# A second expert's operands prepared a block ahead, and four inverse half-products moved, in a spectral layer with two experts

## The chip, the cores and the metric

The kernel runs on one core of a Trainium2 chip. The metric is the time of one execution on the device in microseconds (us); the kernel before takes 1209.12 us, the median of 3 runs (1208.78 to 1209.31). PE is the matrix engine (PEld its weight loads), DVE the vector engine, ACT the scalar engine, POOL the GpSimd engine; SP only issues transfers.

## The reference

Two parts follow each other. The first takes x (2 x 3008 x 256), transforms it along the 3008 positions, multiplies by a complex matrix, shrinks the result towards zero and transforms back. The second sends all 6016 tokens through two dense experts with a hidden width of 2048.

```python
X = rfft(x, axis=1)
Yr = X.real @ w_r - X.imag @ w_i + b_r
Yi = X.real @ w_i + X.imag @ w_r + b_i
Y = sign(Y) * max(abs(Y) - 0.01, 0)          # real and imaginary part each
x = irfft(Y, n=3008, axis=1).reshape(6016, 256)
h = x @ moe_w_in;   x = (h - tanh(h)) @ moe_w_out
h = x @ moe2_w_in;  return (h * clip(h + 3, 0, 6) / 6) @ moe2_w_out
```

All is float32. The kernel writes each large float32 product as three products of rounded operands: a value is split into a rounded part (hi, by an ACT copy) and a remainder (lo, by a subtraction on DVE or POOL), and `three_pass` adds hi x hi, hi x lo and lo x hi.

## The kernel before

The front (lines 649 to 787) does the transform in steps A to D. A and B are matmuls into the frequency domain, `linear` the complex matrix, `shrink` the threshold, C and D the way back. A loop over t = 0 to 23 runs `linear(t)`, `dft_c(t-2)` and `dft_b(t+2)` together; C's results go to DRAM and come back by `load_din(i)`, and `dft_d(i, dh)` is one inverse half-product: eight PE matmuls as the trace counts them into one PSUM bank, then an ACT copy (line 419) into one of the four blocks B11, B12, B21, B22 of a token block.

Then come 16 token blocks k: 0 to 7 for the first expert (752 tokens each, two halves of 376) and 8 to 15 for the second (640, then 768 each, halves of 320 and 384). Each block runs 8 groups g, one for each 256 columns of the hidden layer. A group computes the 2 x 2 block product of weights and tokens with seven products instead of eight (p1 to p7), on operands that `op_split` prepares once per token block: b11, b21, t1, t2, b22, t3, t4, where T1 = B12 - B11, T2 = B22 - T1, T3 = B22 - B12, T4 = B21 - T2 come from `op_sub` on POOL. b11, b21, t1 and t2 have two homes, in `cmH` and `cmL`, for even and odd blocks. b22, t3 and t4 have one home each.

The order of the work is written by hand: each engine runs its instructions in the order of the program, and waits are put in for the data. `group` (line 605) issues p1, p2, p5; ACT's copy `s` of p1 (line 616); the nonlinearity `nl` and its split for the group before; then the outputs of the group before in four parts (`outp`) between p6 with p3, p7 and p4. Products p1, p6, p7 and p4 all build up in one PSUM bank `al`: p6 has to wait until `s` is copied, p7 until `su` is (line 628), p4 until DVE has added `c22` (line 637). Between these steps `hook("a")` to `hook("e")` call `super_hook`, which places everything else: weight decoding, loads, stores and the preparation of the next block n = k + 1:

```python
(5,d) T1, T2   (6,a) b11   (6,d) b21   (7,a) t1, T3   (7,b) t2, T4   (7,e) b22
(0,a) of block n: t3      (0,b) of block n: t4
```

Remainders of b11, b21, t1 and t2 run on POOL, those of b22, t3 and t4 on DVE. While block k of the first expert runs, the four half-products of block n are done at hook c of groups 2 to 5; blocks 9 to 15 load their tokens from DRAM (`load_y1`) at hook c of group 1.

`first_group` (line 574) is group 0 of block 0, cut in pieces that run between the last steps of the front, because the front's last two C products and its DVE steps are still under way.

Of the kernel before, what the change touches and what calls it, by code (L numbers as in the profile page):

```python
# [10 lines left out]
F32 = mybir.dt.float32  # L11
F32R = mybir.dt.float32r
# [76 lines left out]
def spectral_moe_kernel(ctx: ExitStack, tc: tile.TileContext, x, w_r, w_i, b_r, b_i,  # L89
# [72 lines left out]
    def w_flush():  # L162
        w_load(ptr["due"])
        ptr["due"] = 0
# [64 lines left out]
    cmH = pb.tile([128, K1 * 128], F32R, name="cmH")  # L229
    cmL = pb.tile([128, K1 * 128], F32R, name="cmL")  # L230
    b22 = [pb.tile([128, 384], F32R, name=f"b22{p}") for p in "hl"]
    bi_all = pb.tile([128, 3 * 4 * D], F32, name="bi_all")
    bi_ring = [bi_all[:, 4 * D * r:4 * D * (r + 1)].rearrange("p (k d) -> p k d", d=D) for r in range(3)]


    at = ctx.enter_context(ExitStack())
# [168 lines left out]
    def load_din(i, t=None):  # L405
        b, q = divmod(i, 8)
        if t is None:
            t = bi_ring[i % 3]
        t = t[0:96]
        sp.dma_start(out=t, in_=s2w[b][:, 4 * q:4 * q + 4, :])  # L410
        din_t[i] = t

    def dft_d(i, dh, tag):
        t = din_t[i]
        p = bank(tag)
        for u in range(4):
            pe.matmul(out=p[:, u * 94:(u + 1) * 94], lhsT=t[:, u, dh * 128:(dh + 1) * 128], rhs=dmt,  # L417
                      start=True, stop=True)
        act.activation(out=xtf[:, 2 * dh + i % 2, 0:NT].rearrange("p (r u) -> p u r", u=4),  # L419
                       in_=p[:, 0:NT].rearrange("p (u r) -> p u r", u=4), func=ACTF.Copy)  # L420

# [5 lines left out]
    def op_sub(k, out, a, b, eng=pool):  # L427
        eng.tensor_tensor(out=blkv(k, out), in0=blkv(k, a), in1=blkv(k, b), op=ALU.subtract)  # L428

    def op_hi(k, nm):  # L430
        src, slot = OPS[nm]
        n = span[k][1]
        if slot is not None:
            o = 1536 * (k % 2) + NM * slot
            h, l = cmH[:, o:o + n], cmL[:, o:o + n]
        elif nm == "b22":
            h, l = (t[:, 0:n] for t in b22)
        else:
            h, l = (mo["w"].tile([128, NM], F32R, tag=nm + p, name=nm + p)[:, 0:n] for p in "hl")
        act.activation(out=h, in_=blkv(k, src), func=ACTF.Copy)  # L440
        opnd[k, nm] = (h, l)
# [7 lines left out]
        op_lo(k, nm, eng)  # L449

    def early_slot(i):
        return bi_all[:, NT * i:NT * (i + 1)]

    def wt(tag, nt, n=1):
        return mo["w"].tile([128, NM], F32, tag=tag, bufs=n, name=tag)[:, 0:nt]
# [22 lines left out]
    def product(k, g, nm, dst, start):  # L478
        blk, op = PROD[nm]
        w = W["1i" if k < NS else "2i", g]  # L480
        h, l = opnd[k, op]
        sl = slice(blk * 128, (blk + 1) * 128)
        three_pass(dst, w[:, 0, sl], w[:, 1, sl], h, l, start, True, skip_group_check=True)
# [80 lines left out]
    def tail_nl(stage):  # L564
# [5 lines left out]
        else:  # L570
            nl_split(k, g, 1, 0, pend.pop("g"))
            pend.pop("c21")

    def first_group():
        al, be, ga = (bank(t)[:, 0:NT] for t in ("al", "be", "ga"))
        s1, c11, s5, c12, c22 = (early_slot(i) for i in range(5))
        product(0, 0, "p1", al, True)
        product(0, 0, "p2", ga, True)
        product(0, 0, "p5", be, True)
        act.activation(out=s1, in_=al, func=ACTF.Copy)  # L580
        dve.tensor_tensor(out=c11, in0=ga, in1=s1, op=ALU.add)
        act.activation(out=s5, in_=be, func=ACTF.Copy)
        yield
        nl(0, c11, True)
        yield
        product(0, 0, "p6", al, False)
        product(0, 0, "p3", be, False)
        act.activation(out=s1, in_=al, func=ACTF.Copy)
        dve.tensor_tensor(out=c12, in0=be, in1=s1, op=ALU.add)
        yield  # L590
        op_split(0, "t3")
        product(0, 0, "p7", al, False)
        op_hi(0, "t4")
        dve.tensor_tensor(out=c22, in0=al, in1=s5, op=ALU.add)
        op_lo(0, "t4")
        product(0, 0, "p4", al, False)
        nl(0, c12, True)
        nl_split(0, 0, 0, 0, c11)
        nl(0, c22, True)
        nl_split(0, 0, 0, 1, c12, pool)  # L600
        yield
        nl_split(0, 0, 1, 1, c22)
        pend["c21"] = (0, 0, al)
# [45 lines left out]
    with tc.manual_schedule():  # L649
# [61 lines left out]
        for t in range(NP):  # L711
            linear(t)
            if t > 1:
                dft_c(t - 2)
            if t + 2 < NP:
                dft_b(t + 2)
            ab = dft_a(a_next, False) if a_next < 16 else None
            if t > 1:
                evict_c(t - 2)
            if t + 2 < NP:  # L720
                evict_b_hi(t + 2)
            shrink(t)
            if t < NP - 1:
                shrink_hi(t)
            if t + 2 < NP:
                evict_b_lo(t + 2)
            if t == NP - 1:
                first = first_group()
                next(first)
                shrink_hi(t)  # L730
            if t + 2 < NP:
                evict_b_neg(t + 2)
            for _ in range(3 if t < 10 else 2):
                if t > 1 and ptr["dec"] < NDEC:
                    w_step()
            shrink_lo(t)
            for nm in {20: ("b11", "b21"), 21: ("t1",), 22: ("t2", "b22")}.get(t, ()):
                op_lo(0, nm)
            if t == 20:
                op_sub(0, "T1", "B12", "B11", dve)  # L740
            if t == 21:
                op_sub(0, "T2", "B22", "T1", dve)
            if ab:
                dft_a_out(a_next, ab)
                a_next += 1
            flush_stores()
            if t % 2 == 0:
                load_bm(t // 2 + 2)
                load_cm(t // 2 + 1, s_t[t][0].bitcast(F32)[0:1, 0, 0:1])
            if t > 0:  # L750
                load_x(10 + t)
            if t == 0:
                w_load()
            if t % 2 == 1:
                load_bi((t + 1) // 2 + 2)
            w_flush()
            for _ in range(3 if t < 10 else 1 + t % 2):
                if t > 1 and ptr["dec"] < NDEC:
                    w_step()
            if t == 14:  # L760
                load_din(0, din0)
            if t == 15:
                load_din(1, x1[2])
            if t in (17, 18):
                dft_d(0, t - 17, "h")
            if t in (19, 20):
                dft_d(1, t - 19, "h")
            for nm in {19: ("b11", "b21"), 20: ("t1",), 21: ("t2", "b22")}.get(t, ()):
                op_hi(0, nm)
            if t == 22:  # L770
                op_sub(0, "T3", "B22", "B12", dve)
                op_sub(0, "T4", "B21", "T2", dve)

        next(first)
        dft_c(NP - 2)
        next(first)
        evict_c(NP - 2)
        flush_stores()
        dft_c(NP - 1)
        w_flush()  # L780
        at.close()
        mo["w"] = ctx.enter_context(tc.tile_pool(name="mw", bufs=1, reuse_waits="tile"))
        next(first)
        evict_c(NP - 1, bi_all[:, 6 * NT:6 * NT + 512].rearrange("p (k d) -> p k d", k=2))
        flush_stores()
        for _ in first:
            pass

        def super_hook(k, g, pos):
            n = k + 1  # L790
            if g == 0:
                if pos == "a":
                    op_split(k, "t3")
                if pos == "b":
                    op_split(k, "t4")
                if pos == "d":
                    finish(k - 1, 0)
                if pos == "e":
                    finish(k - 1, 1)
            if pos == "a":  # L800
                flush_stores()
            if n < 2 * NS:
                if n < NS:
                    if g == (k == 0) and pos == "c":
                        load_din(2 * n)
                        load_din(2 * n + 1)
                    if 2 <= g < 6 and pos == "c":
                        dft_d(2 * n + (g - 2) // 2, g % 2, "ga")
                elif g == 1 and pos == "c":
                    load_y1(n)  # L810
                if g == 5 and pos == "d":
                    op_sub(n, "T1", "B12", "B11")
                    op_sub(n, "T2", "B22", "T1")
                if g == 6 and pos == "a":
                    op_split(n, "b11", pool)
                if g == 6 and pos == "d":
                    op_split(n, "b21", pool)
                if g == 7 and pos == "a":
                    op_split(n, "t1", pool)
                    op_sub(n, "T3", "B22", "B12")  # L820
                if g == 7 and pos == "b":
                    op_split(n, "t2", pool)
                    op_sub(n, "T4", "B21", "T2")
                if g == 7 and pos == "e":
                    op_split(n, "b22")
            if 1 <= g < 6 and k < NS:
                if pos in "bcd" or pos == "a" and (k == 0 or g % 2):
                    if k or ptr["dec"] < 16:
# [56 lines left out]
```

## Time and profile before

| | |
|---|---|
| median of 3 runs | 1209.12 us |
| the profiled execution | 1207.54 us |
| its span, first to last instruction | 1205.7 us |
| PE busy | 1185.2 us (98%) |
| PEld busy | 1166.4 us (97%) |
| DVE busy | 962.7 us (80%) |
| ACT busy | 875.2 us (73%) |
| POOL busy | 158.7 us (13%) |
| mean granted TensorE clock | 0.995 |

The front ends at about 170 us, the first expert at about 691 us. Matmul records overlap, since a matmul of 376 columns starts every 0.17 us and is shown 0.34 us long; a short hole is therefore seen better in the weight loads, and in the distance between starts, than in PE's busy time.

### The profile page before, as it was taken

How to read it: one execution, taken by the hardware profiler on the slowest of the kernel's cores; microseconds unless marked ns; L12 is line 12 of the kernel's file. 1: busy time of each engine (PE TensorE's matmuls, PEld its weight loads, DVE VectorE, ACT ScalarE, POOL GpSimd, SP SyncE). 2: the span in 40 equal slices, each digit the busy share in tenths (PEclk: the TensorE clock that was granted, in tenths of full speed). 3: DMA queues.
4: the chain of work that ended last, by engine and by line, in shares of the span. 5: the costliest groups of instructions: out<-in, count | busy, mean ns of one | idle time of the engine just before them, and what ended most of it. 6: DMA issues, size and time to landing. Idle time of an engine off the chain costs nothing.

```text
span 1205.7 us, 20883 instructions
## 1 busy us (share of the span) xinstructions
PE 1185.2 (98%) x7806; PEld 1166.4 (97%) x7806; DVE 962.7 (80%) x1818; ACT 875.2 (73%) x1828; POOL 158.7 (13%) x162
## 2 busy tenths in 40 slices
PE   8999999999999999999999999999999999999998
PEld 6899989999999999999999999999999999999997
DVE  2599988888988888888777788778787878787875
ACT  2586768777777777777777677777777777777775
POOL 1010000203020110202021402020200202020200
PEclk9899999999999999999999999999999999999999
DMA  8996522112222223120105530101010101010000
GB/s 274 289 315 230 175 86 64 37 54 75 103 95 75 74 75 105 53 88 20 52 1 185 183 117 1 49 2 53 1 54 1 54 1 53 1 43 12 16 13 27
DMA packets 49149, 96.52 MB, mean 80 GB/s; under 512 B 4424, under 2 KB 28072, under 8 KB 49048
## 3 DMA queue, kind: packets, MB, share of 16 engines
q1 hardware_dynamic: 43078, 74.09, 19.2%
q0 software_dynamic: 4032, 14.68, 3.9%
q10 hardware_dynamic: 1938, 6.42, 1.5%
q8 instruction: 61, 1.00, 0.4%
q14 instruction: 40, 0.33, 0.1%
HBM read 58.22 MB, written 36.44 MB: 79 GB/s over the span
## 4 chain that ended last, share of the span: by engine, by line
PE 73%; DVE 10%; ACT 9%; DMA 5%; issue 2%; SPq 0%; ACTq 0%; DVEq 0%
PE acc L120 13%; PE acc L122 12%; PE acc L121 12%; PE al L120 7%; PE al L121 6%; PE al L122 6%; PE be L120 3%; PE be L122 3%; PE be L121 3%; DMA xb<-in_x_dram 3%; ACT gh L116 2%; PE ga L417 2%; DVE g L463 2%; PE ga L120 2%; PE ga L122 2%
## 5 line engine op out<-in xcount | busy, mean ns | idle before, releaser
L117 DVE TENSOR_TENSOR gl<-g,gh 128x376 fp32r<-128x376 f32 (+2 forms) x509 | 290.9, 571 | 149.1 <-ACT gh L116 123.3
L116 ACT ACTIVATE gh<-g 128x376 fp32r<-128x376 f32 (+2 forms) x509 | 263.0, 517 | 176.1 <-DVE g L466 91.9
L121 PE MATMUL acc<-wo,gh 128*128 128x256 f32 x752 | 211.7, 282 | 0.0
L120 PE MATMUL acc<-wo,gh 128*128 128x256 f32 x752 | 211.5, 281 | 0.0
L122 PE MATMUL acc<-wo,gl 128*128 128x256 f32 x752 | 211.1, 281 | 0.0
L120 PE MATMUL acc<-gh,wo 128*128 128x376 f32 x512 | 173.8, 339 | 0.0
L122 PE MATMUL acc<-gh,wo 128*128 128x376 f32 x512 | 171.1, 334 | 0.0
L121 PE MATMUL acc<-gl,wo 128*128 128x376 f32 x512 | 170.8, 334 | 0.0
L122 PEld LDWEIGHTS acc<-wo,gl 128*128 128x128 f32 x752 | 142.7, 190 | 0.0
L121 PEld LDWEIGHTS acc<-wo,gh 128*128 128x128 f32 x752 | 141.9, 189 | 0.0
L120 PEld LDWEIGHTS acc<-wo,gh 128*128 128x128 f32 x752 | 141.7, 188 | 0.0
L428 POOL TENSOR_TENSOR bmt<-bmt 128x376 f32<-128x376 f32 (+2 forms) x60 | 74.2, 1237 | 458.2 <-ACT bmt L419 332.2
L466 DVE SCALAR_TENSOR_TENSOR g<-e,c 128x384 f32<-128x384 f32 (+1 forms) x192 | 119.6, 623 | 11.8 <-ACT e L465 6.4
L465 ACT ACTIVATE e<-c,three 128x384 f32<-128x384 f32 (+1 forms) x192 | 116.7, 608 | 8.2 <-DVE c L630 8.0
L463 DVE TENSOR_TENSOR g<-c,e 128x376 f32<-128x376 f32 x189 | 114.1, 604 | 6.1 <-ACT e L462 3.3
L445 POOL TENSOR_TENSOR cmL<-bmt,cmH 128x376 fp32r<-128x376 f32 (+2 forms) x60 | 64.8, 1081 | 308.2 <-ACT cmH L440 308.2
L462 ACT ACTIVATE e<-c 128x376 f32<-128x376 f32 x189 | 97.4, 516 | 10.3 <-DVE c L630 10.2
L120 PEld LDWEIGHTS acc<-gh,wo 128*128 128x128 f32 x512 | 96.3, 188 | 0.0
L121 PEld LDWEIGHTS acc<-gl,wo 128*128 128x128 f32 x512 | 96.2, 188 | 0.0
L122 PEld LDWEIGHTS acc<-gh,wo 128*128 128x128 f32 x512 | 96.1, 188 | 0.0
L620 ACT ACTIVATE s<-be 128x376 f32<-128x376 f32 (+2 forms) x127 | 61.7, 486 | 39.7 <-PE be L122 38.4
L120 PE MATMUL al<-cmH,wi 128*128 128x376 f32 (+2 forms) x256 | 87.7, 343 | 2.4 <-ACT s L616 2.0
(182 smaller groups left out, 2843.5 us busy)
## 6 DMA issues: line engine op xcount, KB each, us to landing
raw<-in_moe_w_in_dram SPq DMA_DIRECT2D x16, 512.0 KB
raw<-in_moe_w_out_dram SPq DMA_DIRECT2D x16, 512.0 KB
w2id<-wout SPq DMA_DIRECT2D x8, 896.0 KB
wi<-w2id POOLq DMA_DIRECT2D x8, 896.0 KB, 4.8
y1d<-y SPq DMA_DIRECT2D x32, 188.0 KB
s<-co SPq DMA_DIRECT2D x23, 256.0 KB
bi_all<-s SPq DMA_DIRECT2D x11, 512.0 KB
bi_all<-s SPq DMA_DIRECT2D x14, 384.0 KB
```

The source lines that it names most:

```text
L116: act.activation(out=hi, in_=src, func=ACTF.Copy)
L117: (lo_eng or dve).tensor_tensor(out=lo, in0=src, in1=hi.bitcast(F32), op=ALU.subtract)
L120: pe.matmul(out=out_ap, lhsT=lh, rhs=rh, start=start, stop=False, **kw)
L121: pe.matmul(out=out_ap, lhsT=lh, rhs=rl, start=False, stop=False, **kw)
L122: pe.matmul(out=out_ap, lhsT=ll, rhs=rh, start=False, stop=stop, **kw)
L428: eng.tensor_tensor(out=blkv(k, out), in0=blkv(k, a), in1=blkv(k, b), op=ALU.subtract)
L445: (eng or dve).tensor_tensor(out=l, in0=blkv(k, OPS[nm][0]), in1=h.bitcast(F32), op=ALU.subtract)
L462: act.activation(out=e, in_=src, func=ACTF.Tanh)
L463: dve.tensor_tensor(out=g, in0=src, in1=e, op=ALU.subtract)
L465: act.activation(out=e, in_=src, func=ACTF.Relu, bias=three)
L466: dve.scalar_tensor_tensor(out=g, in0=e, scalar=6.0, in1=src, op0=ALU.min, op1=ALU.mult)
L620: act.activation(out=s5, in_=be, func=ACTF.Copy)
```

## The change

Four edits. (1) b22 gets a second home for odd blocks, and in the first expert its split moves from hook (7,e) to (6,e). (2) For blocks 9 to 15, b22, t3 and t4 have second homes in odd blocks; all seven splits are placed in groups 2 to 6 of the block before (`prep`), all with their remainders on POOL, and `load_y1` moves to group 0. (3) The four half-products of block 1 leave groups 2 to 5 of block 0: three are issued between the last pieces of the front, the fourth inside `first_group`. The two of i = 3 are only multiplied there, and their ACT copies run at hook a of group 1. Their inputs are loaded at t = 16 and t = 21 into tiles that held x. (4) The ring `bi_all` becomes three tiles, so that the second homes can follow in their place; the front's last C result goes to a tile of the experts' pool.

```diff
-    bi_all = pb.tile([128, 3 * 4 * D], F32, name="bi_all")
-    bi_ring = [bi_all[:, 4 * D * r:4 * D * (r + 1)].rearrange("p (k d) -> p k d", d=D) for r in range(3)]
+    bi_ring = [pb.tile([128, 4, D], F32, tag=f"ring{r}", name=f"bi{r}") for r in range(3)]
+    second = {}
...
+        elif k % 2 and (nm == "b22" or k > NS):
+            if nm not in second:
+                r = ("t3", "t4", "b22").index(nm)
+                second[nm] = pb.tile([128, 2, 512], F32R, tag=f"ring{r}", name=nm + "s")
+            h, l = (second[nm][:, i, 0:n] for i in range(2))
         elif nm == "b22":
...
         op_split(0, "t3")
         product(0, 0, "p7", al, False)
+        ahead.append(dft_d_mm(3, 1, "acc"))
         op_hi(0, "t4")
...
+            if t == 16:
+                load_din(2, x1[1])
+            if t == 21:
+                load_din(3, x1[2])
...
         next(first)
         dft_c(NP - 2)
+        for dh in range(2):
+            dft_d(2, dh, "acc")
         next(first)
         evict_c(NP - 2)
         flush_stores()
         dft_c(NP - 1)
+        ahead.append(dft_d_mm(3, 0, "acc"))
...
-        evict_c(NP - 1, bi_all[:, 6 * NT:6 * NT + 512].rearrange("p (k d) -> p k d", k=2))
+        evict_c(NP - 1, mo["w"].tile([128, 2, D], F32, tag="wout", name="cl"))
...
+        def prep(n, g, pos):
+            if pos == "a" and g == 4:
+                op_sub(n, "T1", "B12", "B11")
+            if pos == "a" and g == 5:
+                op_sub(n, "T2", "B22", "T1")
+                op_sub(n, "T3", "B22", "B12")
+            if pos == "e" and g == 5:
+                op_sub(n, "T4", "B21", "T2")
+            nm = {(2, "d"): "b11", (3, "d"): "b21", (4, "d"): "t1", (5, "d"): "t2",
+                  (6, "a"): "b22", (6, "c"): "t3", (6, "e"): "t4"}.get((g, pos))
+            if nm:
+                op_split(n, nm, pool)
+        def prep_early(n, g, pos):      # as before, but for b22
...
+            nm = {(6, "a"): "b11", (6, "d"): "b21", (6, "e"): "b22"}.get((g, pos))
+            if nm:
+                op_split(n, nm, None if nm == "b22" else pool)
...
-                if pos == "a":
+                if pos == "a" and k <= NS:
                     op_split(k, "t3")
-                if pos == "b":
+                if pos == "b" and k <= NS:
                     op_split(k, "t4")
...
+                if k == 0:
+                    if g == 1 and pos == "a":
+                        for dh in range(2):
+                            dft_d_out(3, dh, ahead[dh])
...
-                elif g == 1 and pos == "c":
+                elif g == (n <= NS) and pos == "c":
                     load_y1(n)
...
-                if g == 7 and pos == "e":
-                    op_split(n, "b22")
+                if n > NS:
+                    prep(n, g, pos)
+                else:
+                    prep_early(n, g, pos)
```

NS is 8. `dft_d_mm` and `dft_d_out` are the two halves of `dft_d`: the matmuls, and the ACT copy.

## Rows read from the trace of the kernel before

**Rows 1.** The page, part 1: busy us, share of the span, instructions.

```profile
PE 1185.2 (98%) x7806; PEld 1166.4 (97%) x7806; DVE 962.7 (80%) x1818; ACT 875.2 (73%) x1828; POOL 158.7 (13%) x162
```

**Rows 2.** Waits from 160 us on: who for whom, us in total, times, longest.

```profile
PEld al L120 <- ACT s L616: 6.7, 16, 1.0
```

**Rows 3.** PE in the second expert, p6 of five groups: start, us, instruction.

```profile
748.66 0.45 PE L120 MATMUL al<-cmH,wi 128*128 128x384 f32 x1 [0.83 <-ACT s L616]
...
828.94 0.34 PE L120 MATMUL al<-cmH,wi 128*128 128x384 f32 x1
...
836.90 0.34 PE L120 MATMUL al<-cmH,wi 128*128 128x384 f32 x1
...
877.03 0.44 PE L120 MATMUL al<-cmH,wi 128*128 128x384 f32 x1 [0.16 <-ACT s L616]
...
941.30 0.44 PE L120 MATMUL al<-cmH,wi 128*128 128x384 f32 x1 [0.16 <-ACT s L616]
```

**Rows 4.** PE in the first expert: p6 of four groups, and one half-product.

```profile
194.58 1.03 PE L417 MATMUL ga<-dmt,bi_all 96*128 96x94 f32 x8
195.39 0.42 PE L120 MATMUL acc<-gh,wo 128*128 128x376 f32 x1
...
565.22 0.44 PE L120 MATMUL al<-cmH,wi 128*128 128x376 f32 x1
...
631.36 0.44 PE L120 MATMUL al<-cmH,wi 128*128 128x376 f32 x1
...
654.88 0.33 PE L120 MATMUL al<-cmH,wi 128*128 128x376 f32 x1
...
662.62 0.34 PE L120 MATMUL al<-cmH,wi 128*128 128x376 f32 x1
```

**Rows 5.** ACT at the change into block 11.

```profile
875.62 0.51 ACT L440 ACTIVATE b22h<-bmt 128x384 fp32r<-128x384 f32 x1
...
876.50 0.48 ACT L616 ACTIVATE s<-al 128x384 f32<-128x384 f32 x1
```

**Rows 6.** DVE in block 10, groups 2 and 7.

```profile
831.50 1.15 DVE L466 SCALAR_TENSOR_TENSOR g<-e,c 128x384 f32<-128x384 f32 x1
...
833.87 0.56 DVE L466 SCALAR_TENSOR_TENSOR g<-e,c 128x384 f32<-128x384 f32 x1
...
872.44 0.55 DVE L637 TENSOR_TENSOR c<-al,s 128x384 f32<-128x384 f32 x1
...
873.73 1.37 DVE L466 SCALAR_TENSOR_TENSOR g<-e,c 128x384 f32<-128x384 f32 x1
```

**Rows 7.** POOL in the same two groups.

```profile
829.82 2.42 POOL L428 TENSOR_TENSOR bmt<-bmt 128x384 f32<-128x384 f32 x2 [19.40 <-DMA bmt<-y1d]
...
872.06 1.33 POOL L445 TENSOR_TENSOR cmL<-bmt,cmH 128x384 fp32r<-128x384 f32 x1
873.35 1.33 POOL L428 TENSOR_TENSOR bmt<-bmt 128x384 f32<-128x384 f32 x1
```

**Rows 8.** Two stretches: length, busy PE, PEld, DVE, ACT, POOL; clock, DMA share, GB/s.

```profile
164.50:166.20 1.70, 0.07 (x1) 0.00 (x0) 1.42 (x3) 0.61 (x2) 0.00 (x0) 1.00 0.00 0
169.90:172.90 3.00, 3.00 (x9) 2.89 (x10) 2.13 (x5) 2.23 (x6) 0.98 (x1) 0.50 0.01 3
```

**Rows 9.** PE: p4 of groups 0 and 1 of block 0.

```profile
169.87 0.65 PE L120 MATMUL al<-t4h,wi 128*128 128x376 f32 x1 [0.73 <-DVE bi_all L594]
...
179.17 0.33 PE L120 MATMUL al<-t4h,wi 128*128 128x376 f32 x1
```

**Rows 10.** ACT in the front and in group 1 of block 0.

```profile
148.11 0.86 ACT L419 ACTIVATE bmt<-ga 128x376 f32<-128x376 f32 x1
148.76 0.92 ACT L440 ACTIVATE cmH<-bmt 128x376 fp32r<-128x376 f32 x2
...
166.53 0.46 ACT L588 ACTIVATE bi_all<-al 128x376 f32<-128x376 f32 x1
...
175.26 0.48 ACT L628 ACTIVATE su<-al 128x376 f32<-128x376 f32 x1 [0.26 <-PE al L122]
```

More of the change, by code (lines that the diff above doesn't have):

```diff
@@ L407, in load_din @@
         if t is None:
-            t = bi_ring[i % 3]
+            t = bi_ring[i % 2]
         t = t[0:96]
@@ L413, in dft_d, with dft_d_mm @@
     def dft_d(i, dh, tag):
+        dft_d_out(i, dh, dft_d_mm(i, dh, tag))
+    def dft_d_mm(i, dh, tag):
         t = din_t[i]
@@ L418, in dft_d, with dft_d_out @@
                       start=True, stop=True)
+        return p
+    def dft_d_out(i, dh, p):
         act.activation(out=xtf[:, 2 * dh + i % 2, 0:NT].rearrange("p (r u) -> p u r", u=4),
@@ L451, in early_slot @@
     def early_slot(i):
-        return bi_all[:, NT * i:NT * (i + 1)]
+        return bi_ring[i // 2].rearrange("p k d -> p (k d)")[:, NT * (i % 2):NT * (i % 2 + 1)]
     def wt(tag, nt, n=1):
@@ L572, in tail_nl @@
             pend.pop("c21")
+    ahead = []
     def first_group():
@@ L787, in spectral_moe_kernel @@
             pass
+        def prep(n, g, pos):
[11 more added lines that the diff above has]
+        def prep_early(n, g, pos):
+            if (g, pos) == (5, "d"):
+                op_sub(n, "T1", "B12", "B11")
+                op_sub(n, "T2", "B22", "T1")
+            if (g, pos) == (7, "a"):
+                op_split(n, "t1", pool)
+                op_sub(n, "T3", "B22", "B12")
+            if (g, pos) == (7, "b"):
+                op_split(n, "t2", pool)
+                op_sub(n, "T4", "B21", "T2")
+            nm = {(6, "a"): "b11", (6, "d"): "b21", (6, "e"): "b22"}.get((g, pos))
+            if nm:
+                op_split(n, nm, None if nm == "b22" else pool)
         def super_hook(k, g, pos):
@@ L802, in super_hook @@
             if n < 2 * NS:
-                if n < NS:
-                    if g == (k == 0) and pos == "c":
+                if k == 0:
+                    if g == 1 and pos == "a":
+                        for dh in range(2):
+                            dft_d_out(3, dh, ahead[dh])
+                elif n < NS:
+                    if g == 0 and pos == "c":
                         load_din(2 * n)
@@ L808, in super_hook @@
                         dft_d(2 * n + (g - 2) // 2, g % 2, "ga")
-                elif g == 1 and pos == "c":
+                elif g == (n <= NS) and pos == "c":
                     load_y1(n)
[L811 to L823, printed above, removed]
-                if g == 7 and pos == "e":
-                    op_split(n, "b22")
+                if n > NS:
+                    prep(n, g, pos)
+                else:
+                    prep_early(n, g, pos)
             if 1 <= g < 6 and k < NS:
```

## The prediction

> **What bounds the kernel now.** I read the busy times first: PE works 98% of the span [rows 1], so only two things can shorten it, less PE work or fewer PE holes. Then I read the waits of PEld, because a hole shows first on the weight load that stands in front of a late matmul. After the front the largest by far is one wait: the weight load of a product into `al` waits for ACT's copy `s` (line 616), 16 times for 6.7 us, the longest 1.0 us [rows 2]. The rows at 748.66, 877.03 and 941.30, which name that wait, are each the first group of a new token block [rows 3]; followed in the order of time, 14 of the 16 are the changes into blocks 1 to 7 and 9 to 15. So the holes sit at the block changes, and in the front just before the first expert.
>
> What one block change costs is read from the starts of product p6 (first `al` matmul after the first outputs). In the second expert two neighbouring groups are 836.90 - 828.94 = 7.96 us apart, a whole block is 941.30 - 877.03 = 64.27 us, and 64.27 - 8 x 7.96 = 0.59 us is lost per block [rows 3]. At 748.66 (block 9, behind the short block 8 of 320 tokens) PE shows 0.83 us idle where the later changes show 0.16 [rows 3], so this one costs 0.59 + 0.67 = about 1.3 us. In the first expert a group is 662.62 - 654.88 = 7.74 us, an inverse half-product (`dft_d`) takes 195.39 - 194.58 = 0.81 us to the next matmul and that one is 0.08 us late, 0.89 us in all; a block with four of them is 631.36 - 565.22 = 66.14 us, so 66.14 - 8 x 7.74 - 4 x 0.89 = 0.66 us is lost per block [rows 4].
>
> Why ACT is late there: just before `s` it runs the `b22h` copy (875.62, then a tanh-like step, then `s` at 876.50) [rows 5], and it came late to that copy because DVE's `g` took 1.37 us where it takes 0.56 alone [rows 6], beside the last two of four POOL operations in a row (872.06 and 873.35, 1.33 us each) [rows 7].
>
> **The change, part by part.** *b22 a group earlier (all blocks).* One ACT copy (two steps of ACT there take 876.50 - 875.62 = 0.88, so 0.44 us for one [rows 5]) and one DVE subtract leave the block change for the end of group 6. In groups 6 and 7 `s` waits for PE, not PE for `s`: none of the 16 waits [rows 2] is in group 7, so 0.44 us is covered there. The 0.66 us of a change falls on two products, p6 (for `s`) and p7 (for t3). I give each half, an estimate: then `s` is 0.33 us late, and with 0.44 us less on ACT it is early by 0.1 us. In blocks 1 to 8 t3 and t4 stay in group 0, on ACT and DVE; they move up with ACT by the same 0.44 us, and p7 by 0.3 us, so p7 should just not wait: a margin of 0.1 us. If that cover is missing, a third of the 0.66 us stays. Bounds for the 7 changes into blocks 1 to 7: 1.5 us (p6 alone, partly) to 7 x 0.66 = 4.6 us; I take three quarters, 3.3 us. The change into block 8 has no such wait; between none and 0.6 us I take 0.2.
>
> *t3, t4, b22 of blocks 9 to 15 prepared a block ahead, remainders on POOL.* Nothing of the operand work is left in groups 7 and 0 but t4's remainder on POOL at the start of group 7, so neither the four-in-a-row nor the extra ACT copies reach the change: 6 x 0.59 = 3.5 us, and 1.3 us for block 9. What it adds is three POOL subtracts per block (1.2 to 1.3 us each [rows 7]) and a denser stretch in groups 4 to 6. POOL's queue is in order, and a subtraction that waits for nothing runs right behind its forerunner: t1's remainder, T2 and T3 run as one chain of some 3.9 us behind group 4, then t2's remainder and T4. The nearest row for such a chain is the pair at 829.82, 2.42 us long [rows 7]; DVE's `g` beside it took 1.15 us [rows 6], and the group around it (828.94 to 836.90) is the one that gave the 7.96 us [rows 3]. That pair cost PE nothing, the chain of four with an ACT copy behind it cost 0.59. A chain of three lies between, and behind it no change follows; I take zero, with 0.3 us per block (2 us) as the other end, and below nothing no gain, since the operations are only added there. The load of y1 moves one group earlier; the tile it writes was last read in group 7 or before, so it waits for nothing.
>
> Beside that: DVE's `c` (line 637), which reads PSUM, took 0.55 us beside POOL, and `g`, which reads two SBUF tiles, took 1.37 [rows 6]. The Trainium skill's page "SBUF — State Buffer", section "Who interferes with whom", says that such a DVE operation and a GpSimd operation that reads SBUF exclude each other for a whole instruction. The rows agree; by that rule alone each POOL operation more may hold up one DVE operation, which is the third rival.
>
> *Half-products of the second block to the front.* Four `dft_d` leave groups 2 to 5 of block 0: 4 x 0.89 = 3.56 us of PE time gained, if the front holds them for nothing. The front has the hole: PE works 0.07 of 1.70 us from 164.5 on [rows 8], since `dft_c(23)` waits for ACT's `sh` until past 166.2, and p4 waits until 169.87 [rows 9]. The first two (1.78 us, before p6 and p3) fill the first hole almost exactly; their two ACT evictions (0.86 us long, the next start 148.76 - 148.11 = 0.65 later [rows 10]) push ACT's copy of 166.53 [rows 10] and all behind it by 1.3 us. The third needs an `acc` bank that `evict_c(22)`, the step behind that copy, frees at about 168.8 (167.8 plus 0.4 and 0.6); it runs to 169.7, p7 follows, the fourth lies under DVE's c22, and p4 starts near 171.2 instead of 169.87. But the granted clock was 0.50 from 169.9 to 172.9 [rows 8], 1.2 GHz, after PE had idled; with the holes mostly filled I expect full clock, and the 9 matmuls counted there, 3.0 / 9 = 0.33 us each, take 7.74 / 45 = 0.17: 1.4 us back. So the first output product starts when it did. Then the bill: in group 1 ACT is still 1.4 us late and now has the third and fourth evictions (1.3 us) ahead of `su`, which ran at 175.26 [rows 10]; and the second pair of `acc` banks that the output product needs is held by them until about 177.2. `su` ends near 177.5, p7 starts near 177.9, and p4 of group 1 near 180.5 instead of 179.17 [rows 9]: 1.3 us lost. T1 and T2 now also run on POOL in this group, beside a DVE that does weight decoding: 0.3 us. Net 3.56 - 1.6 = 2.0 us; bounds -0.5 us (clock low again, 1.4, and a further 1.1 of ACT backlog) and 3.6 us. The two loads moved to SP's queue at t = 16 and 21 write tiles whose readers are done, and stand ahead only of stores and loads needed some 10 us later: nothing.
>
> **The sum.** 3.3 + 0.2 + 3.5 + 1.3 + 2.0 = 10.3 us. The profiled execution took 1207.54 us (span 1205.7), so it would take 1197.2; the median of 1209.12 lies 1.6 us above it, so 1198.8 us.
>
> **Rivals.** *A, the stall only moves (14%).* The chain of three with t1h, or t2's with b22h, does to a group inside the block what the chain of four did to the change. For: same operations, same DVE line. Against: the free pair at 829.82. Then the 4.8 us of blocks 9 to 15 are not saved: 1203.6 us. *B, the front gives nothing and p7 keeps its wait for t3 (14%).* For: ACT and DVE have no slack in group 1, and t3 stays where it was up to block 8. Against: the hole of 1.70 - 0.07 = 1.63 us is there [rows 8]. Without 2.0 and half of 3.3: 1202.5 us. *C, slower (5%).* In blocks 9 to 15 the place is DVE's `g` and `gl`: 11 POOL operations a block instead of 8, and up to 1.37 - 0.55 = 0.8 us for each. It decides once more than (10.3 / 7) = 1.5 us per block of these 11 x 0.8 = 8.8 us reaches PE; with 2 us reaching it the time is 1198.8 + 14 = 1213. Against: eight such operations a block, with three ACT copies at the change, now cost 0.59 [rows 3]. *D, the second homes or the earlier loads wait for their old users*, so that nothing moves (3%): 1209. 64% stay for the forecast, whose own range is 1195 to 1202.
>
> **How the numbers follow.** Best case: 3.6 in the front, 4.6, 0.4 and 4.8 make 13.4, plus the clock beyond my share, about 1194.5 us. Above, A and B belong in; together they reach 1207, but one alone stays under 1204. Range 1194.5 to 1204. A measurement tells 0.2% (2.4 us) from no change: forecast, A and B are faster by that: 0.91; within 0.05; slower 0.04.
>
> **What would show it.** In the trace after: no PEld wait for `s` at block changes 9 to 15, and the distance of p6 over a block 63.7 us there and 65.5 in blocks 1 to 7; `dft_d` at 163.4 and the stretch behind 169.9 at clock 1.00; a wait of 1 to 1.5 us in group 1 of block 0. Wrong: new PEld waits in groups 4 to 6 of blocks 8 to 14 (A, C), p7 waiting for t3 in blocks 1 to 7 (B), or clock 0.5 behind 169 us.

## The result, and the profile after

The changed kernel takes 1199.28 us, the median of 6 runs (1197.74 to 1202.5); the kernel before took 1208.95 in the runs beside it (1208.56 to 1213.51). The ratio is 0.9916, 95% interval 0.9901 to 0.993: 8.5 to 12.0 us less, where 10.3 were forecast. The profiled execution of the changed kernel is its longest run, 1202.5 us with a span of 1200.7, only 5.0 us under the span before. Where that comes from is the first thing to read, or every later stage looks 3.8 us worse than it is.

The page of the changed kernel, part 1, answers to [rows 1]; below it is a line of its part 5 (count, then busy us, mean ns of one, idle before).

```profile
PE 1181.7 (98%) x7806; PEld 1165.6 (97%) x7806; DVE 941.2 (78%) x1797; ACT 879.2 (73%) x1828; POOL 178.6 (15%) x183
...
L477 DVE SCALAR_TENSOR_TENSOR g<-e,c 128x384 f32<-128x384 f32 (+1 forms) x192 | 105.6, 550 | 16.2 <-ACT e L476 11.6
```

POOL got the 21 subtractions (3 for each of blocks 9 to 15) that DVE lost. Though POOL works more, DVE's `g` in the second expert is now 550 ns on the mean, and none of the 192 above takes more than 560. At the end of block 10, where [rows 6] had 1.37 us, the changed kernel's DVE shows:

```profile
871.00 0.56 DVE L477 SCALAR_TENSOR_TENSOR g<-e,c 128x384 f32<-128x384 f32 x1
872.87 0.55 DVE L477 SCALAR_TENSOR_TENSOR g<-e,al 128x384 f32<-128x384 f32 x1
...
875.19 0.56 DVE L477 SCALAR_TENSOR_TENSOR g<-e,c 128x384 f32<-128x384 f32 x1
```

The waits of PEld from 165 us on (who for whom, us in total, times, longest) answer to [rows 2]:

```profile
PEld al L120 <- ACT s L630: 1.6, 5, 0.5
PEld al L120 <- DVE c L651: 1.6, 4, 0.7
PEld acc L120 <- ACT bmt L425: 1.3, 2, 1.1
```

From 6.7 us in 16 waits, the wait for `s` (now line 630) is down to 1.6 in 5, all of them before 692 us; in the second expert PEld waits for nothing. `acc` waiting for `bmt` is new: the price of the moved half-products. PE at p6 in the second expert, for [rows 3]:

```profile
747.63 0.34 PE L120 MATMUL al<-cmH,wi 128*128 128x384 f32 x1
...
874.62 0.34 PE L120 MATMUL al<-cmH,wi 128*128 128x384 f32 x1
...
882.57 0.34 PE L120 MATMUL al<-cmH,wi 128*128 128x384 f32 x1
...
938.30 0.34 PE L120 MATMUL al<-cmH,wi 128*128 128x384 f32 x1
```

No row has a wait behind it. A block is 938.30 - 874.62 = 63.68 us, which is 8 x 7.96: the change of block costs nothing. In the first expert, for [rows 4], a block is 631.96 - 566.28 = 65.68 us instead of 66.14:

```profile
566.28 0.34 PE L120 MATMUL al<-cmH,wi 128*128 128x376 f32 x1
...
631.96 0.34 PE L120 MATMUL al<-cmH,wi 128*128 128x376 f32 x1
```

The end of the front, for [rows 8] and [rows 9]: the granted clock stays at full, and p4 of groups 0 and 1 starts at 175.02 and 184.46. In the first fence (windows) the numbers behind the length are busy PE, PEld, DVE, ACT and POOL, then the clock. The second is PE, the third ACT.

```profile
168.00:177.00 9.00, 7.95 (x51) 6.85 (x50) 6.42 (x13) 6.04 (x13) 0.16 (x1) 1.00 0.08 29
...
176.00:179.00 3.00, 3.00 (x19) 2.84 (x18) 2.13 (x5) 3.00 (x8) 0.99 (x1) 1.00 0.26 88
```

```profile
175.02 0.41 PE L120 MATMUL al<-t4h,wi 128*128 128x376 f32 x1
...
180.50 0.44 PE L120 MATMUL acc<-gh,wo 128*128 128x376 f32 x1 [0.75 <-ACT bmt L425]
...
184.46 0.44 PE L120 MATMUL al<-t4h,wi 128*128 128x376 f32 x1
...
197.82 0.44 PE L120 MATMUL al<-t3h,wi 128*128 128x376 f32 x1
...
208.96 0.44 PE L120 MATMUL al<-t4h,wi 128*128 128x376 f32 x1 [0.41 <-DVE c L651]
```

```profile
179.61 1.51 ACT L425 ACTIVATE bmt<-acc 128x376 f32<-128x376 f32 x2
180.92 0.52 ACT L642 ACTIVATE su<-al 128x376 f32<-128x376 f32 x1
```

**The ledger.** The last C product of the front, `dft_c(23)`, starts at 166.27 us before and at 170.07 after, and all of these 3.8 us are lost before 85 us, where matmuls wait for the first loads. Over all profiles below it starts anywhere from 166.07 to 172.06, in kernels with and without the two added loads. So I count from this product on. (k,g) is p6 of group g of block k; the distances are in us, from one profile each. The last two columns are the time after `dft_c(23)` that the clock was at 1.2 GHz in the profile, and the range of the whole-run mean clock over the kernel's runs.

| kernel | c23 to (0,6) | to (7,1) | to (8,7) | to (9,2) | to (15,2) | c23 to end | at half clock | mean clock, all runs |
|---|---|---|---|---|---|---|---|---|
| before | 50.64 | 422.48 | 101.14 | 24.13 | 385.59 | 1039.40 | 3.4 | 0.991-0.995 |
| after | 49.86 | 419.85 | 100.91 | 22.48 | 382.08 | 1030.56 | 0 | 0.996-0.997 |
| e0_after | 49.83 | 419.74 | 100.85 | 22.46 | 382.08 | 1030.35 | 0 | 0.995-0.997 |
| e1_halves | 50.31 | 422.46 | 101.43 | 24.12 | 385.77 | 1039.46 | 3.4 | 0.994-0.996 |
| e4_no_halves | 51.89 | 419.78 | 100.70 | 22.48 | 382.08 | 1032.31 | 6.8 | 0.993-0.994 |
| e5_two | 52.24 | 420.02 | 100.70 | 22.46 | 382.08 | 1032.90 | 6.8 | 0.993-0.995 |
| e2_b22 | 51.85 | 419.82 | 101.07 | 24.11 | 382.83 | 1035.08 | 6.8 | 0.993-0.994 |
| e7_chain | 51.43 | 422.51 | 101.01 | 22.46 | 382.08 | 1034.91 | 6.8 | 0.993-0.995 |
| e6_dve | 50.34 | 419.80 | 100.91 | 22.55 | 382.08 | 1031.05 | 3.4 | 0.992-0.997 |
| e10_dummy | 50.02 | 419.78 | 100.70 | 22.48 | 382.08 | 1030.32 | 0 | 0.995-0.997 |
| e8_dveout | 49.64 | 420.10 | 100.70 | 22.48 | 382.08 | 1030.40 | 0 | 0.996-0.997 |
| e9_gate | 49.63 | 420.39 | 100.70 | 22.47 | 382.08 | 1030.67 | 3.4 | 0.994-0.997 |
| e12_hold | 48.86 | 420.35 | 100.70 | 22.46 | 382.08 | 1029.84 | 0 | 0.996-0.997 |
| e11_pool2 | 49.87 | 419.86 | 103.30 | 23.32 | 384.15 | 1035.87 | 0 | 0.996-0.997 |

From before to after, column by column: 0.78 + 2.63 + 0.23 + 1.65 + 3.51 = 8.80 us. To these belongs a part that the one profile of before hides: its run had a mean clock of 0.995, while the 45 runs of that kernel beside the experiments have 0.9936 on the mean, which says some 0.0014 x 1209 / 0.5 = 3.4 us more at half clock. PE does 11 matmuls there where it does 19 at full clock (e4_no_halves below), so I estimate that this is worth 3.4 x 8 / 19 = 1.4 us. 8.8 and 1.4 make 10.2, where the two medians are 9.7 apart. The mean clock does not tell where in a run the half clock lay.

### The profile page after: what moved, and what is told of

Its sections match the earlier page's. It is cut to its first block, busy times and chain, and to the rows that moved or that the text cites. A ratio compares the mean times of both kernels' runs of the same rounds, so it can differ in the third digit from the quotient of the medians.

```text
span 1200.7 us, 20891 instructions
## 1 busy us (share of the span) xinstructions
PE 1181.7 (98%) x7806; PEld 1165.6 (97%) x7806; DVE 941.2 (78%) x1797; ACT 879.2 (73%) x1828; POOL 178.6 (15%) x183
## 4 chain that ended last, share of the span: by engine, by line
PE 80%; DVE 9%; ACT 6%; DMA 2%; issue 2%; SPq 1%; ACTq 0%; DVEq 0%
PE acc L120 14%; PE acc L121 14%; PE acc L122 14%; PE al L120 7%; PE al L121 7%; PE al L122 7%; PE be L120 3%; PE be L121 3%; PE be L122 3%; PE ga L120 2%; PE ga L420 2%; PE ga L122 2%; PE ga L121 2%; DVE g L474 1%; ACT gh L116 1%
## 5 line engine op out<-in xcount | busy, mean ns | idle before, releaser
L477 DVE SCALAR_TENSOR_TENSOR g<-e,c 128x384 f32<-128x384 f32 (+1 forms) x192 | 105.6, 550 | 16.2 <-ACT e L476 11.6
```

Source lines behind the costliest of these rows:

```text
L477: dve.scalar_tensor_tensor(out=g, in0=e, scalar=6.0, in1=src, op0=ALU.min, op1=ALU.mult)
```

## The experiments

Each edit is against the changed kernel. Times are medians, ratios are to the kernel before on the same chip.

**e0_after**: the changed kernel as it is.

> The changed kernel again, as it is. Its profiled execution had the front's last C product 3.8 us later than in the kernel before, all of it lost before 85 us, while the rest was 8.8 us faster. If that delay is chance (it lies on loads that the change doesn't touch), another profile shows another value, between 0 and 4 us, and the time is some 1198 to 1200 us, 0.991 of the kernel before. Rival: the change itself delays the front (the ring cut into three tiles, or the added loads); then the delay of 3 to 4 us is there again.

1199.9 us (1198.98 to 1200.7), 0.991 [0.9891, 0.9929]. The result repeats, and here `dft_c(23)` starts at 166.79: the late front of the first profile was no part of the change.

**e1_halves**: the half-products' move alone; operands as before.

```diff
-                if n > NS:
-                    prep(n, g, pos)
-                else:
-                    prep_early(n, g, pos)
+                prep_early(n, g, pos)          # b22 at (7,e), t3 and t4 in group 0
```

> Only the four half-products moved to the front (and the ring cut into three tiles); operands are prepared as in the kernel before. By the trace of the changed kernel from the last C product of the front to group 6 of block 0 this is worth 0.7 us, not the 2.0 that I had forecast: about 1208.2 us. Rival 1: 2.0 us as forecast, and what is missing in that profile is chance: 1207. Rival 2: the move costs the 3.8 us in the front: 1211 to 1212.

1208.2 us (1206.23 to 1210.98), 0.998 [0.9968, 0.9991]: 1.1 to 3.9 us less. In its profile all stretches behind the front are those of before within 0.3 us, block changes included (PEld waits for `s` 6.9 us in 17), and so is the whole from `dft_c(23)` on (1039.46 against 1039.40). What the runs gain goes with their clock, 0.994 to 0.996 against 0.991 to 0.995.

**e4_no_halves**: everything but the half-products' move. The loads, the three issues in the front and the fourth in `first_group` are taken out, and the four `dft_d` are back in groups 2 to 5 of block 0.

> The changed kernel with the four half-products back in groups 2 to 5 of block 0; all operand work as in the change. By the trace the three terms left are 2.6 us for the changes into blocks 1 to 7, 0.3 for block 8, 1.6 for block 9 and 3.5 for blocks 10 to 15, 8.0 us: 1201 us, about 1 us above the changed kernel. Rival 1 (the move is worth 2.0): 2 us above. Rival 2 (the move delays the front): 1198 or less, below the changed kernel, and with less spread between runs.

1201.44 us (1200.75 to 1202.18), 0.9923 [0.9904, 0.9942]. This interval overlaps that of the whole change, so the runs alone don't size the move; the profile does: 51.89 us from `dft_c(23)` to (0,6), 2.0 more than with the move, and the clock falls (windows, PE busy first and clock third from the end):

```profile
167.00:170.00 3.00, 2.14 (x8) 1.49 (x9) 2.16 (x4) 3.00 (x8) 0.00 (x0) 0.93 0.18 66
170.00:173.00 3.00, 2.27 (x7) 1.70 (x7) 2.31 (x5) 1.04 (x4) 0.00 (x0) 0.50 0.06 22
173.00:176.00 3.00, 3.00 (x11) 3.00 (x11) 1.65 (x4) 2.15 (x6) 0.99 (x1) 0.50 0.53 150
```

At half clock PE counts 11 matmuls in 3 us of full work, the changed kernel at full clock 19 (176 to 179 us above).

**e5_two**: only the half-products of i = 2 go to the front, those of i = 3 back to groups 3 and 5.

```diff
-        ahead.append(dft_d_mm(3, 0, "acc"))
...
+                    if g in (3, 5) and pos == "c":
+                        dft_d(3, g // 5, "ga")
```

> The changed kernel, but only the two half-products of i = 2 stay in the front; those of i = 3 are done at hook c of groups 3 and 5 of block 0, in bank ga, as in the kernel before. My reading: the two in the front cost nothing, since they lie in the first hole, and the two others cost as much as they gave, because their ACT copies stand ahead of su in group 1 and hold the two acc banks that the next output product needs (0.9 us wait). So 2 x 0.89 us less what ACT's 1.3 us of delay costs: 0.5 to 1 us faster than the changed kernel. Rival: the loss in groups 3 and 4 of block 0 comes from weight decoding there and stays; then the same time or up to 0.5 us slower.

1202.38 us (1201.31 to 1204.28), 0.9933 [0.9913, 0.9953]: a miss. I had put the bill of group 1 above the gain of the second pair. But without that pair two holes stay open, in front of p7 and p4. The clock falls between them, at about 173.3 us, and is at half all through 174 to 180 us:

```profile
172.55 0.44 PE L120 MATMUL al<-t3h,wi 128*128 128x376 f32 x1 [1.43 <-ACT t3h L451]
...
174.71 0.65 PE L120 MATMUL al<-t4h,wi 128*128 128x376 f32 x1 [0.73 <-DVE bi L607]
```

```profile
174.00:180.00 6.00, 5.29 (x17) 5.22 (x18) 4.10 (x9) 3.64 (x9) 0.99 (x1) 0.50 0.34 105
```

**e10_dummy**: the four half-products stay in groups 2 to 5, and the front multiplies four that nobody reads.

```diff
-            dft_d(2, dh, "acc")
+            dft_d_mm(2, dh, "acc")         # never copied out
```

> The changed kernel with the half-products done in groups 2 to 5 of block 0 as in the kernel before, and, beside that, the same four half-products multiplied in the front with nobody reading the result (so 4 x 0.89 us of PE work more than the kernel before, and no ACT copies in the front or in group 1). It parts two readings of what the move is worth. Without the half-products in the front the granted clock was at half for 6.8 us there, and from the last C product to group 6 of block 0 it took 51.9 us, against 49.8 in the changed kernel. If the worth is the clock alone, the dummies hold it up as well: clock 1.00, and 49.5 to 50.3 us for that stretch, as fast as the changed kernel (1199.5 us). If it is the work that left groups 2 to 5, the stretch takes 51.5 us or more, 1201.5 us or more.

1199.16 us (1198.73 to 1201.12), 0.991 [0.9895, 0.9925]: as good as the change. Its clock is 1.00 from 164 to 179 us. Against e4_no_halves the unread products bring 51.89 - 50.02 = 1.87 us by the clock alone; doing the useful ones there brings 0.16 more. These are single profiles, and the intervals of the runs overlap; the runs' mean clocks do not (0.995 to 0.997 against 0.993 to 0.994).

**e2_b22**: b22 early with its second home in all blocks, t3, t4 and the chain on POOL as before; no move of half-products.

```diff
-         elif k % 2 and (nm == "b22" or k > NS):
+         elif k % 2 and nm == "b22":
...
+                prep_early(n, g, pos)          # for all n, t3 and t4 in group 0
```

> Only b22 moves: a second home for odd blocks and its split at hook (6,e) in all 15 blocks; t1, T3, t2, T4 stay as four POOL operations in a row in group 7, t3 and t4 stay in group 0 on DVE; half-products as in the kernel before. What it tells apart: whether the late s at a change comes from the chain on POOL, from the b22 copy, or needs both. My theory: both add up (s late by about 1.3 us through DVE beside POOL and 0.4 through the copy, against 1.4 us of room), so that taking either away is enough for p6; p7's small wait for t3 may stay. Then 2.9 us in the first expert, as in the changed kernel, 0.4 to 0.6 us per change into blocks 10 to 15 and some 0.5 at block 9: 5.5 to 7 us faster than the kernel before, 1202 to 1203.5 us. Rival: the chain alone decides in the second expert; then nothing is gained there and the time is 1206.

1204.89 us (1203.92 to 1205.53), 0.9955 [0.9941, 0.9969], above what I expected. The first expert has the whole gain (419.82); the changes into blocks 10 to 15 have 2.76 of 3.51 us, and the change into block 9 has none (24.11): the wait for `s` is still there.

```profile
749.51 0.44 PE L120 MATMUL al<-cmH,wi 128*128 128x384 f32 x1 [0.40 <-ACT s L629]
```

**e7_chain**: the opposite. b22, t3 and t4 stay at hooks (7,e), (0,a), (0,b) with one home each; in blocks 9 to 15 only b11, b21, t1, t2 and the four T move to the places of `prep`, so that no four POOL operations run in a row in group 7. No move of half-products.

```diff
-                  (6, "a"): "b22", (6, "c"): "t3", (6, "e"): "t4"}.get((g, pos))
+                  (7, "e"): "b22"}.get((g, pos))
```

> The other half: for blocks 9 to 15 the chain is dissolved (b11, b21, t1, t2 and the four subtractions where the changed kernel has them, y1 loaded in group 0), but b22 stays at (7,e), t3 and t4 in group 0, all three on DVE with one home; first expert and half-products as in the kernel before. My theory (either is enough): p6 no longer waits at changes 9 to 15, 0.45 to 0.59 us each and 1.5 at block 9, so 4.2 to 5 us faster than the kernel before: about 1204.5 us. Rival: the copies at the change are the cause; then the kernel before's time, 1209.

1204.81 us (1202.31 to 1206.61), 0.9956 [0.9941, 0.997]. The second expert has the full gain, 22.46 and 382.08; a block is 942.41 - 878.73 = 63.68 us.

```profile
878.73 0.34 PE L120 MATMUL al<-cmH,wi 128*128 128x384 f32 x1
...
942.41 0.34 PE L120 MATMUL al<-cmH,wi 128*128 128x384 f32 x1
```

The edit also takes the ACT copies of t1 and t2 out of group 7, so the rows have to part the two. Before the change into block 11, from the start of DVE's `g` to the start of the `gh` behind the next `g`, it took 875.19 - 871.45 = 3.74 us in the kernel before (first fence, DVE and ACT) and takes 875.76 - 873.34 = 2.42 here (second fence). The difference of 1.32 us is that of the two `g`: 1.06 and 1.37 [rows 6] against 0.56 and 0.56.

```profile
871.45 1.06 DVE L466 SCALAR_TENSOR_TENSOR g<-e,c 128x384 f32<-128x384 f32 x1 [0.23 <-ACT e L465]
...
875.19 0.53 ACT L116 ACTIVATE gh<-g 128x384 fp32r<-128x384 f32 x1 [1.50 <-DVE g L466]
```

```profile
873.34 0.56 DVE L477 SCALAR_TENSOR_TENSOR g<-e,c 128x384 f32<-128x384 f32 x1 [0.22 <-ACT e L476]
...
875.11 0.56 DVE L477 SCALAR_TENSOR_TENSOR g<-e,c 128x384 f32<-128x384 f32 x1
...
875.76 0.53 ACT L116 ACTIVATE gh<-g 128x384 fp32r<-128x384 f32 x1 [0.68 <-DVE g L477]
```

**e6_dve**: `prep`'s remainders of b22, t3 and t4 on DVE, so that POOL has 8 operations a block as before, not 11.

```diff
-                op_split(n, nm, pool)
+                op_split(n, nm, None if nm in ("b22", "t3", "t4") else pool)
```

> The changed kernel with the remainders of b22, t3 and t4 of blocks 9 to 15 on DVE instead of POOL, at the same places. It tells what the 21 POOL operations that the change adds cost. My theory: nothing on either engine reaches PE there, same time as the changed kernel within 0.5 us. Rival (DVE held up beside POOL already reaches PE): faster by 1 us or more. The other rival (DVE too full): slower by 1 us or more, with new waits of PE in groups 6 and 7.

1201.42 us (1198.69 to 1204.95), 0.993 [0.9915, 0.9945]. From (0,6) on its stretches are those of the change within 0.1 us, so 3 POOL operations more or less make no difference. What this profile loses lies ahead of there, where the edit changes nothing. Its runs spread over 6 us, with mean clocks of 0.992 to 0.997; why their median is higher is not shown.

**e11_pool2**: each of `prep`'s seven remainders is computed twice on POOL, 18 operations a block.

```diff
                 op_split(n, nm, pool)
+                op_lo(n, nm, pool)
```

> The changed kernel with every remainder of blocks 9 to 15 computed twice on POOL, one behind the other: 18 POOL operations per block instead of 11, some 23 us of 64. It asks from where POOL costs PE time. My theory: DVE's room is not used up yet; 0 to 1 us slower, since each pair is like the pair of subtractions that cost nothing. Rival (the port between POOL and DVE decides): each doubled remainder holds one more DVE step up by up to 0.8 us, a group falls behind by more than the 1.4 us of room, and 7 x 0.5 us or more is lost: 1203 us or more.

1205.54 us (1204.72 to 1206.29), 0.9961 [0.9946, 0.9976]: a miss, the rival is right at this load. Some 0.34 us a block goes lost in blocks 10 to 15 ((384.15 - 382.08) / 6) and 3.2 us around block 8. DVE's `g` stands beside POOL again, and `c`, behind it in DVE's queue, makes p4 late: PEld waits for it 4.2 us in 9 over the second expert, and for no operand (DVE in block 10, then the waits of PEld from 690 to 760 us):

```profile
869.46 1.36 DVE L477 SCALAR_TENSOR_TENSOR g<-e,c 128x384 f32<-128x384 f32 x1
```

```profile
PEld al L120 <- DVE c L651: 2.5, 3, 1.0
```

**e8_dveout**: the copies of the half-products of i = 3 run on DVE inside `first_group`, not on ACT in group 1.

```diff
         ahead.append(dft_d_mm(3, 1, "acc"))
+        dft_d_out(3, 0, ahead[0], dve)
...
         nl(0, c22, True)
+        dft_d_out(3, 1, ahead[1], dve)
```

> The changed kernel, but the third and fourth half-product of the front leave PSUM on DVE, inside the first group, where DVE had idle stretches of 0.7 us (behind t3's remainder, and before the last remainder of that group), instead of on ACT at hook a of group 1. Then their two acc banks are free before the output product of group 1 asks for them (0.9 us wait, 0.2 of restarts), su is not behind 1.3 us of copies, and ACT enters groups 2 to 4 of block 0 with less backlog (0.3 and 0.6 us of waits there). My theory: 1 to 2 us faster than the changed kernel, with no wait on the copies of line 425 left. Rival: the waits in groups 3 and 4 come from weight decoding alone; then 0.9 to 1.1 us. Second rival: DVE becomes late for c22 and p4 waits for it; then no gain.

1198.41 us (1198.31 to 1199.4), 0.9906 [0.9893, 0.9919]. The wait of `acc` for `bmt` is gone, yet the stretch shrinks by 0.2 us only: p4 of group 1 now waits for c22. Read upwards: ACT's `gh` waits for `g`, which stood in DVE's queue behind a `gl` of 1.31 us, beside T1 and T2 on POOL. In order of the fences, PE, POOL, DVE, ACT:

```profile
180.22 0.44 PE L120 MATMUL al<-t4h,wi 128*128 128x376 f32 x1 [0.91 <-DVE c L657]
```

```profile
173.78 2.39 POOL L438 TENSOR_TENSOR bmt<-bmt 128x376 f32<-128x376 f32 x2
```

```profile
175.27 1.31 DVE L117 TENSOR_TENSOR gl<-g,gh 128x376 fp32r<-128x376 f32 x1
```

```profile
177.08 0.52 ACT L116 ACTIVATE gh<-g 128x376 fp32r<-128x376 f32 x1 [1.01 <-DVE g L478]
```

**e9_gate**: e8_dveout, and T1 and T2 of block 1 queued behind b11's remainder at hook (6,a) of block 0, so that POOL can't run them in group 1.

```diff
-            if (g, pos) == (5, "d"):
+            if (g, pos) == (5, "d") and n > 1:
...
+            if (g, pos) == (6, "a") and n == 1:
+                op_sub(n, "T1", "B12", "B11")
+                op_sub(n, "T2", "B22", "T1")
```

> As the kernel whose third and fourth half-product leave PSUM on DVE, and T1 and T2 of block 1 are moved behind b11's remainder at hook (6,a) of block 0, so that they no longer run on POOL in group 1. In that kernel they ran from 173.8 to 176.2 us, DVE's remainder beside them took 1.31 us, ACT's next copy waited 1.0 us for DVE, and p4 of group 1 came 1.07 us late. My theory: this wait goes, 0.8 to 1.1 us less between the front's last C product and group 6 of block 0 (49.64 there), so about 48.7, and 1197.5 us. Rival: the weight decoding's two ACT steps in that group (1.2 us) hold p4 up by themselves; then 0.3 us or less.

1201.43 us (1198.86 to 1202.09), 0.9926 [0.9912, 0.994]: a miss. p4's wait is gone and (0,1) to (0,6) falls from 41.28 to 39.75 us, but in this profile the clock fell, and took the 1.5 us back ahead of it:

```profile
171.80:175.20 3.40, 3.40 (x12) 3.40 (x13) 3.28 (x7) 2.56 (x6) 0.99 (x1) 0.50 0.21 73
```

That PE was late by then is part of the fall: with the clock held (e12_hold) the distance is 40.49 us. The profile is also that of the fastest run, so it doesn't explain the median.

**e12_hold**: e9_gate with one more half-product in the front that nobody reads, behind the third half-product.

```diff
         ahead.append(dft_d_mm(3, 0, "acc"))
+        dft_d_mm(2, 1, "acc")
```

> The kernel with T1 and T2 behind b11 and the half-products' copies on DVE, and one more half-product (i = 2 again, result unused, 0.89 us) multiplied between the third half-product and p7, where PE stood idle for 0.7 us. In that kernel the late p4 of group 1 was gone, 39.75 us from p6 of group 1 to p6 of group 6 instead of 41.28, but the granted clock fell to half for 3.4 us at 172 us, which took 1.5 us back. My theory: with this hole filled the clock stays at 1.00 and both gains stand: 48.1 to 48.6 us from the last C product to group 6 (49.8 in the changed kernel), about 1198 us, 1.3 us faster than the changed kernel. Rival: the clock falls none the less, or the longer PE work before p7 costs what it holds; then 49.5 us or more and 1199.5 us or more.

1199.25 us (1198.62 to 1202.96), 0.9915 [0.9902, 0.9929]. The clock holds. The front stretch (48.86, a little short of the 48.1 to 48.6 expected) and the time from `dft_c(23)` to the end (1029.84) are the shortest of all, the latter 0.7 us under the change, but the median can't be told from the change's: runs of one kernel spread by 1 to 6 us here. So no version measurably beats the change.

## Why the prediction was right, and where its steps were not

**The block changes of the second expert** (3.5 + 1.3 forecast): 3.51 and 1.65 measured, 63.68 us a block where 63.7 was named. The changed operations cost nothing, as taken from the pair of [rows 7]. The change into block 9 was undersized, by 0.35 us. The reason was half right. I let the second homes and the chain on POOL go together; e7_chain shows that dissolving the chain brings all of it, and e2_b22 that moving b22 away brings 2.76 of 3.51 and nothing at block 9. The gains don't add: once ACT is not held up by a late `g`, its copies at the change fit. Two readings were loose: of the two POOL operations put beside the `g` at 873.73 only the one from 873.35 overlaps it (the other overlaps the `g` at 871.45), and the ACT step between `b22h` and `s` is a Relu, not tanh-like.

**Rivals A and C** (the stall moves, or POOL holds up DVE): false at 11 operations a block, by the 63.68 us of a block, the 550 ns of `g` and e6_dve. e11_pool2 shows that the mechanism of C is real and sets in between 11 and 18. What decides is whether a wait behind `g` ends last.

**Rivals B and D.** B is false for p7 in five of the seven blocks: from p6 of a block's first group to the next p6 it is 7.79 to 7.82 us instead of 8.04 to 8.06. Only in blocks 3 and 4 it is still 8.00. What B says of the front comes below. D is false: no block change got longer, and PEld waits for nothing in the second expert.

**Blocks 1 to 7** (3.3): 2.63 us. Five changes give 0.44 to 0.48 each, near the 0.47 taken; those into blocks 3 and 4 give 0.26 and 0.11. The four POOL operations in group 7 don't tell them apart: DVE's `g` before the change takes 1.34 or 1.35 us, and ACT's `gh` waits 1.55 or 1.56 for it, at all seven. The step that failed in these two is that b22's copy is covered at the end of group 6. In blocks 2 and 3 ACT runs some 0.6 us later there, in the kernel before as in the changed one, and with b22's copy on ACT and its remainder on DVE added the delay reaches group 7. In block 1 (first two ACT rows) `su` and `s` start 0.76 and 7.05 us behind p6, in block 2 1.06 and 7.32 (PE's p6, then ACT):

```profile
293.36 0.34 PE L120 MATMUL al<-cmH,wi 128*128 128x376 f32 x1
...
359.18 0.34 PE L120 MATMUL al<-cmH,wi 128*128 128x376 f32 x1
```

```profile
294.12 0.47 ACT L642 ACTIVATE su<-al 128x376 f32<-128x376 f32 x1
...
300.41 0.48 ACT L630 ACTIVATE s<-al 128x376 f32<-128x376 f32 x1
...
360.24 0.47 ACT L642 ACTIVATE su<-al 128x376 f32<-128x376 f32 x1
...
366.50 0.48 ACT L630 ACTIVATE s<-al 128x376 f32<-128x376 f32 x1
```

The spare time taken for `s`, an estimate of 0.1 us, was too even over the blocks. Why ACT is later in blocks 2 and 3 stays open, and no run tried whether dissolving the chain would cure these two as well.

**Block 8** (0.2): 0.23 us between the two profiles, but e1_halves, which leaves this change as it was, is 0.29 off as well, so the term is not shown.

**The half-products** (2.0): right in sum, wrong in kind. The details came as forecast: the new wait of `acc` is 1.1 us (1 to 1.5 named); with `dft_c(23)` set to its time of before (3.80 us off the p4 starts and `su` row above), p4 of group 0 starts at 171.22 (171.2 named), `su` ends at 177.64 (177.5), p4 of group 1 starts at 180.66 (180.5). The runs of e1_halves give 1.1 to 3.9 us for the move alone. But I booked it as 4 x 0.89 us of PE work taken away, less a bill of 1.6, and the clock as what merely pays for the later start. Two things differ. Groups 2 to 5 of block 0 give back 2.38 us, not 3.56: p6 is 5.40 us later than before in group 2 and 3.02 in group 6, since p7 of group 3 (197.82) and p4 of group 4 (208.96, waiting for `c`) are late. With 5.40 - 3.80 = 1.60 us of bill, the 1.6 named, 0.78 is left of the work gained. And e10_dummy shows that most of the gain is the clock: unread products in the same place do nearly as well. At the same clock the useful work brings 0.16 us (e10_dummy and after, none at half clock) to 0.33 (before and e1_halves, both 3.4 us). Nor was the one profile of before typical: it has 3.4 us at half clock, whereas the kernels that leave the front as it was have 6.8 in their profiles, and the runs of before a mean of 0.9936. This is why the move seems worth 0.78 us between the two profiles, and 2.0 against e4_no_halves.

The forecast was made from a single execution. Its terms add up to 8.80 us between the two profiles, 1.5 less than forecast; what brings the medians near it is, by the estimate of 1.4 us above, the lower clock of before's other runs, which the forecast did not know of. That the total came out so near is in part luck. What sets the time of `dft_c(23)`, 6 us from profile to profile, stays open.

## What to carry to other kernels

When an in-order engine is late at a boundary, look one queue further back: here ACT was late because DVE was, and DVE because four POOL operations stood in a row; in the second expert spreading those out was enough, and the added buffers were not needed for it. Work moved into a hole of PE can be worth more through the clock than through the work; an unread product in the same hole tells the two apart. Compare two profiles from the first point at which they should agree, not from their start.

## What was not expected of the hardware

The clock's drop behind the front is not fixed by the program: e8_dveout and e9_gate are alike up to group 1 and show none and 3.4 us at 1.2 GHz, e6_dve shows 3.4 at 176 us and 6.8 more at about 77 us. A hole of PE of 1.43 us (e5_two) stood before 6.8 us at half clock; holes of 0.34 and 0.56 us, up to p7 in the changed kernel, were followed by none.
